# Three small cuts in the start-up of a token-mixing kernel: bands in one VectorE instruction, one evacuation moved to ScalarE, a weight load moved to a quiet step

## The chip, the cores and the metric

The kernel runs on one core of one Trainium2 chip. The metric is the device time of one execution in microseconds (us). The program's own span, which the profile counts from, is about 2 us shorter. Single runs of one and the same kernel lie up to some 5 us apart, and a good part of this study is about where that comes from. A "look" below is one profiled execution. To evacuate a tile is to copy a matmul's result out of PSUM, TensorE's accumulators, so that the next operation can use it.

## The reference, cut to what matters

A causal convolution of seven taps with softmaxed weights per head, then a token-mixing block:

```python
x_unf = x_pad[:, idx, :].reshape(B, S, K, H, group)      # B=8, S=4224, K=7, H=8, D=192
x = np.einsum('hk,bskhg->bshg', w, x_unf).reshape(B, S, D)
theta = x @ w_theta                                      # 192 x 192
zr, zi = x * np.cos(theta), x * np.sin(theta)
y = np.einsum('ts,bsd->btd', w_tok_r, zr) + np.einsum('ts,bsd->btd', w_tok_i, zi)   # 4224 x 4224
u = x + y
out = u + np.maximum(u @ w_ch, 0.0)
```

Nearly all arithmetic is in the two token matmuls.

## The kernel before

The tokens are cut into 33 chunks of 128. A chunk goes through `conv` (matmuls with banded weights), `transpose`, `theta` (a matmul and two sines on ScalarE), products and sums (VectorE), and is then one right-hand side of the token matmuls, which run in steps. In the start-up, about 100 us, eleven chunks are prepared while steps 0 to 4 already use those that are ready. After that TensorE is full. Filler matmuls (`idle`) on zeros are meant to raise TensorE's clock early on; "full" and "half" clock below are what the trace records as granted. The parts that the change and the argument touch:

```python
def transpose(self):
    self.xT = turned()
    transposed(self.xT, self.x, range(NG), self.k < 3)   # True: evacuated by VectorE, else ScalarE
...
# in mix(): the token matmuls of one step, seven runs, three PSUM accumulators in two buffers
for r, (wn, zn, cn, opens, to) in enumerate(runs):
    if opens:
        y[cn] = ypool.tile([P, 2, PC], F32, name="y", tag="y")
...
# start of the program, after the softmax of the taps
idle(8)
bp = banks("bp")
for q in range(Q): ...                                   # 32 tiny matmuls spread the taps into bp
bv = bp[0 : 2 * WR, 0, 0 : Q * H].rearrange("p (q h) -> p h q", h=H)
dve(nc.vector.tensor_scalar_mul(
    out=bands[:, :, 0, :], in0=bv, scalar1=block[:, 0:1]
))
act(nc.scalar.activation(
    out=bands[:, :, 1, :], in_=bv, func=AT.Copy, scale=block[:, 1:2]
))
...
# emitted after the eleven chunks of the start-up
dve(nc.vector.memset(wch[:, 1:3, :], 0.0))
for rows, i, part_w in channel_pieces(moe_w_ch):
    nc.gpsimd.dma_start(out=wch[rows, i, :], in_=part_w)
```

## Time and profile before

| | before |
|---|---|
| time, median of the runs made with the changed kernel | 1449.35 us (1445.97 to 1450.87, 4 runs) |
| span of the profiled run | 1449.8 us |
| TensorE idle in that span | 31.8 us |
| first convolution | 9.20 us |
| first sine on ScalarE | 15.94 us |
| end of the start-up: first token matmul after TensorE's last long wait | 103.82 us |

The two lines of the page that matter are the busy shares of the engines and the chain of waits that ended last, by engine:

```profile
PE 1418.0 (98%) x9809; PEld 887.4 (61%) x9809; DVE 976.5 (67%) x1051; ACT 315.2 (22%) x379; POOL 434.2 (30%) x655
...
PE 86%; DVE 5%; DMA 4%; ACT 2%; issue 2%; POOL 1%; SPq 0%; DVEq 0%; ACTq 0%; POOLq 0%
```

TensorE (PE) is busy for 98% of the span, and 86% of the chain is its own. The idle time lies mainly in the start-up (17.5 us before 104 us) and in the last 75 us (9.7 us), with 2.0 us of waits near 600 us. The prediction below shows the start-up's lines.

### The profile page before, as it was taken

The page shows a single profiled execution, that of the slowest core. Times are in us where ns is not written, and L with a number is a line of the kernel's source. Part 1 is how long each engine was busy: PE and PEld are TensorE (multiplying, and loading weights), DVE is VectorE, ACT ScalarE, POOL GpSimd, SP SyncE. Part 2 cuts the span into 40 slices and gives each one's busy share as a digit, 9 for nine tenths or more (in the row PEclk, how much of TensorE's full clock was granted, in tenths as well). Part 3 has the DMA queues.
Part 4 walks back from the last instruction along what each step waited for, and adds up shares of the span by engine and source line. Part 5 has one row for each costly group of instructions (what it writes and reads, how often), then busy time and mean ns, then how long its engine had stood idle before and what let it go on. Part 6 is the DMA issues. An engine that isn't in the chain of part 4 may idle for free.

```text
span 1449.8 us, 23748 instructions
## 1 busy us (share of the span) xinstructions
PE 1418.0 (98%) x9809; PEld 887.4 (61%) x9809; DVE 976.5 (67%) x1051; ACT 315.2 (22%) x379; POOL 434.2 (30%) x655
## 2 busy tenths in 40 slices
PE   7899999999999999999999999999999999999997
PEld 4556666666666666556666666666666666666665
DVE  6883555545448777756665667877777767767686
ACT  6851101111134244000000004434210110010133
POOL 7431211111233232342433342333323123213120
PEclk9999999999999999999999999999999999999999
DMA  9986756465699999988899889989999999999883
GB/s 171 246 164 140 146 101 151 89 149 97 137 232 206 223 249 217 227 222 209 206 267 210 237 143 240 238 184 230 279 216 210 206 200 223 204 204 194 166 227 119
DMA packets 272029, 281.99 MB, mean 195 GB/s; under 512 B 106672, under 2 KB 240176, under 8 KB 271920
## 3 DMA queue, kind: packets, MB, share of 16 engines
q0 software_dynamic: 162464, 92.15, 48.3%
q1 hardware_dynamic: 71824, 178.88, 35.0%
q10 hardware_dynamic: 37632, 9.44, 4.4%
q8 instruction: 77, 1.26, 0.3%
q14 instruction: 32, 0.26, 0.1%
HBM read 245.49 MB, written 108.13 MB: 244 GB/s over the span
## 4 chain that ended last, share of the span: by engine, by line
PE 86%; DVE 5%; DMA 4%; ACT 2%; issue 2%; POOL 1%; SPq 0%; DVEq 0%; ACTq 0%; POOLq 0%
PE y L443 78%; PE v L141 5%; DMA st<-in_moe_w_tok_i_dram 2%; PE pc L210 1%; PE tp L165 1%; DVE pv L408 1%; ACT z L246 1%; DVE z L257 1%; DVE z L251 1%; DVE wt L336 1%; DMA xw<-in_x_dram 1%; DVE wt L348 1%; ACT pv L406 1%; ACT uT L151 0%; DMA part<-pv 0%
## 5 line engine op out<-in xcount | busy, mean ns | idle before, releaser
L443 PE MATMUL y<-z,wt 128*128 128x384 f16 x7656 | 1285.6, 326 | 11.8 <-DVE pv L408 8.7
L443 PEld LDWEIGHTS <-wt 128*128 128x128 f16 x7656 | 741.1, 98 | 491.4 <-issue 14.4
L408 DVE TENSOR_TENSOR pv<-y,pv 128x768 f32<-128x768 f32 x324 | 308.9, 954 | 326.8 <-PE y L443 285.8
L336 DVE STREAM_TRANSPOSE wt<-st 128x1408 f16<-128x1408 f16 (+7 forms) x224 | 327.7, 1465 | 50.6 <-PE y L443 41.1
L323 POOL DMA_DIRECT2D st<-in_moe_w_tok_r_dram x232 | 132.3, 578 | 462.5 <-DVE wt L336 456.6
L323 POOL DMA_DIRECT2D st<-in_moe_w_tok_i_dram x232 | 132.3, 578 | 409.9 <-DVE wt L336 394.4
L348 DVE TENSOR_TENSOR wt<-wt 128x1408 f16<-128x1408 f16 (+7 forms) x216 | 174.1, 806 | 42.0 <-PE y L443 39.6
L151 ACT ACTIVATE z<-pc 128x768 f16<-128x768 f32 x65 | 53.3, 819 | 388.8 <-PE pc L210 388.6
L151 ACT ACTIVATE ub<-pv 128x768 f16<-128x768 f32 x63 | 50.2, 835 | 333.0 <-DVE pv L408 326.6
L406 ACT ACTIVATE pv<-y 128x768 f32<-128x768 f32 x66 | 54.0, 818 | 283.5 <-PE y L443 281.4
L141 PEld LDWEIGHTS <-uT 128*128 128x128 f16 x1056 | 91.5, 98 | 27.8 <-issue 9.0
L386 POOL TENSOR_TENSOR pv<-pv,xr 128x1536 f32<-128x1536 f32 x24 | 74.5, 3103 | 74.6 <-DVE wt L348 31.8
L197 POOL DMA_DIRECT2D xw<-in_x_dram x132 | 76.3, 586 | 26.9 <-DMA xw<-xw 7.5
L476 DVE SCALAR_TENSOR_TENSOR pv<-v,pv 128x768 f32<-128x768 f32 x66 | 62.9, 954 | 27.7 <-PE v L141 27.3
L257 DVE TENSOR_TENSOR z<-z 128x768 f16<-128x768 f16 x132 | 73.4, 556 | 3.6
L151 ACT ACTIVATE uT<-tp 128x1536 f16<-128x1536 f16 (+1 forms) x48 | 58.2, 1215 | 74.7 <-PE tp L165 74.7
L246 ACT ACTIVATE z<-v,half_pi 128x768 f16<-128x768 f32 x66 | 59.8, 906 | 42.5 <-PE v L141 42.1
L251 DVE TENSOR_TENSOR z<-z 128x1536 f16<-128x1536 f16 x66 | 60.1, 947 | 5.7 <-ACT z L246 5.7
L141 PE MATMUL v<-wth,uT 128*128 128x192 f16 x528 | 55.2, 248 | 5.7 <-ACT z L246 3.4
L141 PE MATMUL v<-wch,uT 128*128 128x192 f16 x528 | 54.2, 246 | 2.1 <-DVE pv L476 1.2
L246 ACT ACTIVATE z<-v 128x768 f16<-128x768 f32 x66 | 53.4, 810 | 0.0
L210 PE MATMUL pc<-xw,bands 96*64 96x192 f16 x528 | 35.7, 259 | 1.8 <-ACT bands L625 1.1
(44 smaller groups left out, 140.3 us busy)
## 6 DMA issues: line engine op xcount, KB each, us to landing
part<-pv SPq DMA_DIRECT2D x79, 768.0 KB, 4.3
pv<-part SPq DMA_DIRECT2D x79, 768.0 KB, 6.1
out_dram<-pv SPq DMA_DIRECT2D x66, 384.0 KB, 4.4
st<-in_moe_w_tok_r_dram POOLq DMA_DIRECT2D x136, 176.0 KB, 5.9
st<-in_moe_w_tok_i_dram POOLq DMA_DIRECT2D x136, 176.0 KB, 5.2
xs<-z SPq DMA_DIRECT2D x132, 96.0 KB, 4.2
xw<-in_x_dram POOLq DMA_DIRECT2D x121, 96.0 KB, 5.8
xr<-xs SPq DMA_DIRECT2D x24, 384.0 KB, 4.2
```

Source lines behind the costliest of these rows:

```text
L141: pe(nc.tensor.matmul(v[:, k, b * D : (b + 1) * D], lhsT=tT[:, 3 * k + b + i, :], rhs=w[:, 2 * b + i, :], start=(i == 0), stop=(i == 1),))
L151: act(nc.scalar.activation(out=out, in_=in_, func=AT.Copy))
L197: nc.gpsimd.dma_start(out=self.xw[lo : lo + n, h, :, :], in_=x[:, t0 : t0 + n, :].rearrange("b s d -> s b d"),)
L246: act(nc.scalar.activation(**args))
L251: dve(nc.vector.tensor_tensor(out=o, in0=xv, in1=o, op=ALU.mult))
L257: dve(nc.vector.tensor_tensor(out=z[:, o, :], in0=z[:, a, :], in1=z[:, b, :], op=ALU.subtract))
L323: pool(nc.gpsimd.dma_start(out=st[a * Q : (a + 1) * Q, 0:nb, :, 0:n] .rearrange("i r bt s -> i (r bt) s"), in_=w[self.tbs[0] * P : (self.t ...
L336: dve(nc.vector.transpose(self.w[name][:, 0 : self.n, :, :], self.st[int(name[1])][:, int(name[0]) - 1, :, 0 : self.n * Q] .rearrange("p b ...
L348: dve(nc.vector.tensor_tensor(out=self.w[name][:, 0 : self.n, :, :], in0=self.w[a][:, 0 : self.n, :, :], in1=self.w[b][:, 0 : self.n, :, : ...
L386: ins = pool(nc.gpsimd.tensor_tensor(out=self.pv[i], in0=self.pv[i], in1=self.xr[i], op=ALU.add))
L408: dve(nc.vector.tensor_tensor(out=o, in0=yv, in1=o, op=ALU.add))
L443: pe(nc.tensor.matmul(y[cn][:, q, 0:BH], lhsT=self.w[wn][:, c, :, :].rearrange("p bt i -> p (bt i)"), rhs=chunks[k].z[:, zn, q * BH : (q + ...
```

## The change

The intent is to shorten the start-up in three places: one VectorE instruction in place of a VectorE and a ScalarE instruction in a row, the transposed x of chunk 2 evacuated by ScalarE, which is idle there, and the zeroing and loading of the channel weights taken out of the start-up's full end and put into step 15, where there is room.

```diff
-            transposed(self.xT, self.x, range(NG), self.k < 3)
+            transposed(self.xT, self.x, range(NG), self.k < 2)
...
+        if t == NU - 2:
+            def load_wch():
+                dve(nc.vector.memset(wch[:, 1:3, :], 0.0))
+                for rows, i, part_w in channel_pieces(moe_w_ch):
+                    pool(nc.gpsimd.dma_start(out=wch[rows, i, :], in_=part_w))
+            found.append((3, load_wch))
...
-    dve(nc.vector.tensor_scalar_mul(
-        out=bands[:, :, 0, :], in0=bv, scalar1=block[:, 0:1]
-    ))
-    act(nc.scalar.activation(
-        out=bands[:, :, 1, :], in_=bv, func=AT.Copy, scale=block[:, 1:2]
+    dve(nc.vector.tensor_tensor(
+        out=bands, in0=bv.unsqueeze(2).to_broadcast([2 * WR, H, 2, Q]),
+        in1=block[:, :].unsqueeze(1).unsqueeze(3).to_broadcast([2 * WR, H, 2, Q]),
+        op=ALU.mult,
     ))
...
-    dve(nc.vector.memset(wch[:, 1:3, :], 0.0))
-    for rows, i, part_w in channel_pieces(moe_w_ch):
-        nc.gpsimd.dma_start(out=wch[rows, i, :], in_=part_w)
```

## The prediction

> **What bounds the kernel now.** I read the page's busy shares first, then the busy time of each engine by stretches, then the chain of waits, then the timeline of the few microseconds that the change touches. TensorE is busy for 1418.0 of 1449.8 us, so some 32 us can be lost or won in waits at all. The stretches show where they lie (columns: stretch and length, then busy us and instruction count of PE, PE weight loads, DVE, ACT and POOL, then the granted clock, DMA share, GB/s):
>
> ```profile
> 28.00:60.00 32.00, 26.50 (x244) 17.00 (x242) 26.77 (x43) 27.71 (x35) 17.60 (x32) 0.95 1.29 219
> 60.00:80.00 20.00, 18.41 (x179) 12.62 (x178) 19.26 (x28) 18.26 (x23) 6.80 (x12) 1.00 1.14 255
> 80.00:104.00 24.00, 20.65 (x163) 13.31 (x161) 22.24 (x31) 14.27 (x18) 6.49 (x12) 1.00 0.76 160
> 104.00:421.00 317.00, 317.00 (x1947) 190.28 (x1946) 159.79 (x140) 41.20 (x51) 66.40 (x117) 0.99 0.64 132
> ```
>
> From 104 to 421 us TensorE never waits. Before that there is a start-up of about 100 us in which eleven chunks of x go through convolution, transpose, sine and products while the first token matmuls already run. There ScalarE (27.71 of 32 us between 28 and 60) and then VectorE (22.24 of 24 us between 80 and 104) are the full engines. All three parts of the change remove work from that start-up, so they are worth only what they shorten of it; whatever TensorE gains there should shift the whole full stretch after it, and so the end.
>
> **Part one, the bands.** The timeline at the start:
>
> ```profile
> 8.10 0.48 DVE L622 TENSOR_SCALAR bands<-bp,block 96x256 f16<-96x256 f32 x1 [1.66 <-PE bp L616]
> ...
> 8.68 0.47 ACT L625 ACTIVATE bands<-bp,block 96x256 f16<-96x256 f32 x1 [1.90 <-DVE bands L622]
> ...
> 9.20 1.49 PE L210 MATMUL pc<-xw,bands 96*64 96x192 f16 x16 [1.14 <-ACT bands L625]
> ...
> 13.30 0.50 PEld L210 LDWEIGHTS <-bands 96*64 96x64 f16 x8 [0.20 <-DMA xw<-in_x_dram]
> ```
>
> Today VectorE writes one half of the bands, then ScalarE the other, one after the other (8.10 to 8.58, 8.68 to 9.15), and the first convolution starts at 9.20. After the change one VectorE multiply of 96 x 512 does both. The Trainium skill, "VectorE: DVE Perf Modes", in its perf-mode tier table has a tensor_tensor with a PSUM operand at one element per cycle, and in the section on the TRN2 errata gives (N+151)/0.96 ns for an fp32 tensor_tensor in SBUF. Applied to N = 768 that is 957 ns, and the trace has 954 ns for the 768-wide adds that read PSUM (L408), so it may be used here: N = 512 gives an estimated 0.69 us. Scaling from the 256-wide instruction instead (0.48 us plus 256 elements at 0.96 GHz) gives 0.75. The bands are then ready at 8.10 + 0.69..0.75 = 8.8 to 8.85 instead of 9.15: the first convolution starts **0.30 to 0.35 us earlier**.
>
> But what of it gets through? The last line shows TensorE at 13.30 waiting 0.20 us for a DMA, before the convolution of chunk 1. The instruction order shows the semaphores of that wait: the load of chunk 1 and the copies of its history rows out of chunk 0's tile, neither of which needs the bands. So the 0.3 us turns into a wait of 0.5 us there. The only other user, the evacuation of chunk 0's transposed x, moves earlier on VectorE and saves less than 0.1 us. I put this part at 0 to 0.1 us. The two casts of the theta weights behind it slip by about 0.25 us, to 9.5, and are first needed at 14.69.
>
> **Part two, the transposed x of chunk 2.** The timeline around it:
>
> ```profile
> 25.13 0.80 ACT L246 ACTIVATE z<-v 128x768 f16<-128x768 f32 x1
> ...
> 26.58 0.92 DVE L149 COPY uT<-tp 128x1536 f16<-128x1536 f16 x1
> 26.61 0.81 ACT L151 ACTIVATE z<-pc 128x768 f16<-128x768 f32 x1 [0.68 <-PE pc L210]
> 27.43 1.80 DVE L251 TENSOR_TENSOR z<-z 128x1536 f16<-128x1536 f16 x2
> ...
> 27.56 0.83 PE L141 MATMUL v<-wth,uT 128*128 128x192 f16 x8 [0.98 <-DVE uT L149]
> ...
> 28.43 0.90 ACT L246 ACTIVATE z<-v,half_pi 128x768 f16<-128x768 f32 x1 [1.00 <-PE v L141]
> ```
>
> The transposes are in PSUM at 25.13, but VectorE is busy with sums and a weight transpose and takes the tile only at 26.58. TensorE waits 0.98 us for it and ScalarE 1.00 us behind that. ScalarE is free from 25.93, and the order of the changed kernel puts the evacuation just there, ahead of the convolution output of 26.61. The Trainium skill, "ScalarE: Activation LUTs", section "What ACT_TABLE_LOAD costs", has an ACTIVATE with immediate scale and bias at 186 + 0.833 N ns and back-to-back ones overlapping by about 93 ns; for N = 1536 that is 1.47 us, and the trace has 1.45 to 1.50 us for the same evacuation on ScalarE in later chunks. So it ends at 25.93 + 1.45 = 27.38 to 27.43, against 26.58 + 0.92 = 27.50 on VectorE. The slower engine finishes first, by **about 0.1 us**, because it starts 0.65 us earlier. Its extra 1.35 to 1.45 us fit into the 0.68 + 1.00 = 1.68 us that ScalarE idles now. The displaced convolution output ends at 28.1, which frees its PSUM buffer just as TensorE wants it (28.2). From 28.43 the chain of waits runs mostly over ScalarE and TensorE up to about 58 us, so this 0.1 us should travel on. VectorE gets 0.92 us back, so the products at 27.43 move forward by some 0.8 us; but it idles 1.33 us for ScalarE at 43.60 and 1.80 at 50.35, which eats that. Sum: 0.1 us.
>
> **Part three, the channel weights.** The chain of waits ends its start-up on VectorE:
>
> ```profile
> 101.98 0.76 DVE wt L348
> 102.74 0.21 DVE wch L705
> 102.95 0.82 DVE pv L408
> 103.77 0.05 issue
> 103.82 6.24 PE y L443 x27
> ```
>
> This is the clearest piece. The zeroing of the channel-weight tile takes 0.21 us on a full VectorE immediately before the PSUM add for which TensorE waits 2.46 us. Taking it out lets TensorE resume **0.21 us earlier**, and TensorE does not wait again for 300 us. The four loads that hang on the memset blocked the GpSimd queue for 5.63 us, but the token-weight load behind them then waits 1.03 us more for a weight transpose anyway, so nothing is gained there. In their new place, step 15 (about 366 to 391 us), the queue stands idle: the trace has
>
> ```profile
> 387.42 2.28 POOL L323 DMA_DIRECT2D st<-in_moe_w_tok_i_dram  x4 [12.93 <-DVE wt L336]
> ```
>
> so 12.93 us of idle swallow four issues of 0.55 us = 2.2 us, and VectorE, idle for some 2 us between instructions there, swallows a 0.22 us memset. The Trainium skill, "DMA: Bandwidth & Descriptors", section "SWDGE vs HWDGE vs iDMA", says a cast during a DMA can only be issued from GpSimd, which is why this fp32 to fp16 load sits in that queue; the trace agrees (all wch issues are POOL's), and no other queue is tried here. The weights are first read at 1063 us. They could hardly be late.
>
> **Sum.** 0.05 + 0.1 + 0.21 = 0.36, so about **0.4 us of 1448, or 0.03%**. From the median of 1448.21 that is 1447.8.
>
> **Rivals.** First, **a new wait in the SyncE queue**. The built order shows one thing that the diff does not: the first load of x rows for the final sum (xr, 384 KB) moves from the 86th place of SyncE's queue to the 38th, ahead of the history copies of chunks 5 and 6, and it waits there for chunk 3's rows to land in DRAM. I estimate chunk 5's copies at 35.4 to 37.8 us instead of 32.45 to 34.9; with the 4.8 us from issue to landing that this stretch shows they are there at 42.6, and TensorE wants them at 44.3. DMA is full in this stretch, so the margin of under 2 us may not hold; a miss would cost perhaps 1 us, at most 3. It also rotates the semaphores and adds one or two waits to ScalarE's first accumulator copies (the trace has about 0.08 us for each). Second, **ScalarE as the tighter bound**: it is the fullest engine from 28 to 60 us and gets 1.35 us more. If the evacuation started later than 25.93, the convolution output behind it would hold the next matmuls and the part would lose up to 0.5 us. Against it stands the idle of 1.68 us. Third, **the gain is larger**: the earlier VectorE work could remove several later waits of TensorE, and the whole could reach 1.5 us. Against it: between 28 and 80 us ScalarE, not VectorE, ends most of the waits. Fourth, **everything is swallowed** but the memset, or even that, by a later wait (589 to 636 us on the token-weight loads): those start when TensorE lets VectorE transpose, so they should move with it.
>
> **Range and chances.** None of these reaches 29 us, which is what 2% would be. The regime-wise reading agrees with the Trainium skill, "Perfetto Trace Analysis", section "Optimization Strategy" (the most contended engine changes over time): only a stretch of 100 us is touched, and most of it is left as it is. The range is therefore mostly that of the runs: three of the same kernel span 1445.97 to 1450.87, 4.9 us, ten times my effect. I take 1445.3 to 1450.3. Faster by over 2%: 0.3%; slower: 0.7%.
>
> **What would show it.** Right: one bands instruction of 0.69 to 0.75 us and the first convolution at about 8.9; a longer DMA wait, near 0.5 us, before chunk 1's convolution; the evacuation of chunk 2 on ScalarE at 25.9 and the theta matmuls at 27.45; TensorE's last start-up wait ending at about 103.4; the wch issues near 380 us with no new TensorE wait. Wrong: a TensorE wait for a DMA near 44 us, a start-up ending after 103.8 or before 102.8, or TensorE waits between 104 and 421 us. The trace may well show the 0.4 us where the run times cannot.

## The result, and the profile after

| | before | after |
|---|---|---|
| median of 4 runs | 1449.35 us (1445.97 to 1450.87) | 1448.3 us (1446.65 to 1450.9) |
| span of the profiled run | 1449.8 us | 1444.6 us |
| first convolution | 9.20 | 8.89 |
| first sine | 15.94 | 14.74 |
| end of the start-up | 103.82 | 102.48 |

The ratio is 0.9998 with a 95% interval of 0.9973 to 1.0022: the same. A ratio is the mean time of one kernel's runs over that of the other's of the same rounds, so it is not quite the ratio of the medians.

But the two profiled runs differ by 5.2 us, 14 times what was predicted, and that needs an explanation before any part of it is credited to the change. The lines of the changed kernel that answer to those of before, first the page:

```profile
PE 1414.5 (98%) x9809; PEld 886.3 (61%) x9809; DVE 978.2 (68%) x1050; ACT 316.2 (22%) x379; POOL 434.6 (30%) x655
...
PE 89%; DVE 3%; DMA 2%; ACT 2%; POOL 1%; issue 1%; SPq 0%; DVEq 0%; ACTq 0%; POOLq 0%
```

The bands and what follows, from the timeline:

```profile
8.16 0.69 DVE L628 TENSOR_TENSOR bands<-bp,block 96x512 f16<-96x512 f32 x1 [1.66 <-PE bp L622]
...
8.89 1.49 PE L210 MATMUL pc<-xw,bands 96*64 96x192 f16 x16 [0.78 <-DVE bands L628]
...
12.68 0.52 PE L210 MATMUL pc<-xw,bands 96*64 96x192 f16 x8
```

The instruction takes 0.69 us, as estimated, and the first convolution starts 0.31 us earlier. The convolution of chunk 1, which was to wait 0.5 us for a DMA, waits for nothing and is 0.62 us earlier than before.

The transposed x of chunk 2:

```profile
24.62 1.45 ACT L151 ACTIVATE uT<-tp 128x1536 f16<-128x1536 f16 x1
...
25.95 0.82 ACT L151 ACTIVATE z<-pc 128x768 f16<-128x768 f32 x1
26.13 0.83 PE L141 MATMUL v<-wth,uT 128*128 128x192 f16 x8 [0.75 <-ACT uT L151]
...
27.00 0.90 ACT L246 ACTIVATE z<-v,half_pi 128x768 f16<-128x768 f32 x1 [0.23 <-PE v L141]
```

ScalarE takes it right behind the previous sine. The end of the start-up, from the chain of waits (start, length, engine and line), now without the memset:

```profile
100.80 0.76 DVE wt L348
101.55 0.88 DVE pv L408
102.43 0.05 issue
102.48 7.65 PE y L443 x46
```

And the channel weights in their new place, in the timeline; the bracket says for what GpSimd had waited before the line:

```profile
376.03 0.22 DVE L531 MEMSET wch<- 128x192 uint32 x1
376.55 1.61 POOL L533 DMA_DIRECT2D wch<-in_moe_w_ch_dram  x3 [4.47 <-DVE wch L531]
...
384.41 2.32 POOL L323 DMA_DIRECT2D st<-in_moe_w_tok_i_dram  x4 [6.25 <-DVE wt L336]
```

GpSimd still waits 6.25 us for VectorE afterwards, and TensorE has no wait between 104 and 421 us. So the move is hidden.

What then makes 5.2 us? Three pieces can be read off. The start-up ends 1.34 us earlier. Between 570 and 640 us the kernel before waited 1.97 us for token weights, and the changed one did not. The remaining 1.9 us lie mostly just after the start-up, and the stretches there show what they are (columns as in the prediction; the first number after POOL's count is the granted clock). The kernel before:

```profile
12.00:15.00 3.00, 3.00 (x25) 2.14 (x24) 1.59 (x3) 0.81 (x1) 3.00 (x6) 0.50 1.28 170
...
104.50:107.50 3.00, 3.00 (x11) 1.36 (x10) 2.04 (x3) 0.00 (x0) 2.16 (x4) 0.50 0.39 37
```

and the changed kernel:

```profile
12.00:15.00 3.00, 2.83 (x35) 1.96 (x35) 1.93 (x4) 1.07 (x2) 3.00 (x6) 0.95 1.34 180
...
104.50:107.50 3.00, 3.00 (x20) 1.80 (x19) 3.00 (x4) 0.26 (x1) 1.78 (x4) 1.00 0.84 108
```

In both stretches the kernel before ran at half the TensorE clock, 0.50 where the other has 0.95 and 1.00. In the second it did 11 matmuls in the time of 20. The clock record of the traces is a row of windows of 3.413 us each, at full or at half speed. Before: half from 8.66 to 15.48 (two windows), from 35.96, and from 104.23. After: half from 8.87 to 12.28 (one window) and from 36.17. So two fewer half-speed windows. Is that the change, or chance?

### The profile page after: what moved, and what is told of

Read it like the earlier page. It is cut to its first block, busy times and chain, and to the rows that moved or that the text cites. A ratio compares the mean times of both kernels' runs of the same rounds, so it can differ in the third digit from the quotient of the medians.

```text
span 1444.6 us, 23749 instructions
## 1 busy us (share of the span) xinstructions
PE 1414.5 (98%) x9809; PEld 886.3 (61%) x9809; DVE 978.2 (68%) x1050; ACT 316.2 (22%) x379; POOL 434.6 (30%) x655
## 4 chain that ended last, share of the span: by engine, by line
PE 89%; DVE 3%; DMA 2%; ACT 2%; POOL 1%; issue 1%; SPq 0%; DVEq 0%; ACTq 0%; POOLq 0%
PE y L443 81%; PE v L141 5%; PE pc L210 1%; PE tp L165 1%; ACT z L246 1%; DVE pv L408 1%; DMA xw<-xw 1%; POOL xw L197 1%; DMA xw<-in_x_dram 1%; DVE z L257 1%; POOL st L323 1%; DVE z L251 1%; DMA pv<-part 1%; ACT uT L151 1%; DVE wt L336 0%
## 5 line engine op out<-in xcount | busy, mean ns | idle before, releaser
L348 DVE TENSOR_TENSOR wt<-wt 128x1408 f16<-128x1408 f16 (+7 forms) x216 | 176.1, 815 | 40.5 <-PE y L443 38.0
```

Source lines behind the costliest of these rows:

```text
L348: dve(nc.vector.tensor_tensor(out=self.w[name][:, 0 : self.n, :, :], in0=self.w[a][:, 0 : self.n, :, :], in1=self.w[b][:, 0 : self.n, :, : ...
```

## The experiments

**Theory A**: the parts of the change set the start-up, and a second look at either kernel gives the same figures. **Theory B**: the boundaries of the clock windows lie elsewhere in each run, so which windows come out at half speed is partly chance; the parts are worth a few tenths each on top. A third question is whether the bands' 0.31 us passes on or is swallowed by a DMA, as predicted.

Looks compare stretches of one trace, not total times.

### A second look at the kernel before

No edit.

> The kernel before, unchanged, a second look. In the first look its clock record has half-speed windows of 3.41 us: two in a row from 8.66 us, one at 35.96, one at 104.23; the start-up ended at 103.82 and the first ScalarE sine at 15.94. Theory A (the parts of the change alone set the start-up): the same figures within 0.1 us. Theory B (the clock windows lie where they happen to, and their number differs from run to run): the phase of the windows is different, the number of half-speed windows before 110 us need not be four, and the first sine lies between 14.9 (one early window) and 16.0 (two), the start-up end moving with it.

Measured: span 1446.4 us, 3.4 us less than the first look at the same program, and its first sine and start-up end differ by 0.22 and 0.46 us. Theory A is out. The bands matmuls took 2.64 us in place of 1.57, because the fillers had not raised the clock by then; full clock came at 13.88 us. First convolution 10.28, first sine 16.16, start-up end 104.28, all later than in the first look. But no half-speed window followed at 104 us and there was no wait near 600. The first sine is 0.16 us above the expected range of 14.9 to 16.0: the early clock has more than the two cases that were thought of.

### One part at a time

```diff
 bands only : tensor_scalar_mul + activation  ->  one tensor_tensor        (rest as before)
 xT only    : self.k < 3  ->  self.k < 2                                   (rest as before)
 wch only   : memset and loads moved to step 15                            (rest as before)
```

> Before plus part one only (one VectorE instruction for the bands). Theory A (prediction): first convolution 0.31 us earlier (8.9), but the convolution of chunk 1 waits for a DMA until about 13.3, first sine at 15.9, start-up end 103.7 to 103.8. Theory C (the 0.31 us passes through because no DMA gates chunk 1): chunk 1 at 13.0 with equal clock, first sine 15.6, start-up end about 103.5. Theory B (an early half-speed window lost or kept decides): first sine near 14.8 if only one early half-speed window is recorded, near 15.6 to 15.9 if two.

> Before plus part two only (transposed x of chunk 2 evacuated by ScalarE). Prediction: up to the second chunk nothing changes; the interval from the first sine of chunk 1 to the first sine of chunk 2 (21.82 to 28.43 in the first look, 6.61 us) becomes about 6.5 by the prediction, 6.38 as the look at the changed kernel had it. Both theories: by chunk 3 (first look: sine at 39.77, that is 17.95 after chunk 1's) the changed kernel had lost it again (17.95): if the loss belongs to the part, it is lost here too.

> Before plus part three only (channel weights loaded in step 15). From the last sine of the start-up (93.17) to the first matmul after the last start-up wait (103.82) it takes 10.65 us in the first look. Prediction: 10.44, as the memset of 0.21 us is gone; the changed kernel had 10.50. Rival (the memset had slack): 10.65. Nothing at 370 to 380 us makes TensorE wait.

Measured, bands only: first convolution 8.85, chunk 1 at 12.66 with no DMA wait, first sine 14.72, start-up end 102.86. One early half-speed window, as theory B had it; whether the 0.35 us as such passes on is told below, by all looks together.

Measured, transposed x only: from the second sine of chunk 1 to the first sine of chunk 2 it takes 3.87 us (24.78 to 28.65). The second look at before has 4.10 (24.55 to 28.65), bands only 4.10, wch only 4.10, and the changed kernel 3.87. The lines of the second look at before and of xT only, in this order:

```profile
26.80 0.92 DVE L149 COPY uT<-tp 128x1536 f16<-128x1536 f16 x1
...
28.65 0.90 ACT L246 ACTIVATE z<-v,half_pi 128x768 f16<-128x768 f32 x1 [1.00 <-PE v L141]
```

```profile
26.27 1.45 ACT L151 ACTIVATE uT<-tp 128x1536 f16<-128x1536 f16 x1
...
28.65 0.90 ACT L246 ACTIVATE z<-v,half_pi 128x768 f16<-128x768 f32 x1 [0.23 <-PE v L141]
```

So the part gains **0.23 us**; all eight looks at the changed kernel and its variants have 3.86 or 3.87. The old place can cost more: in w_before (below), where VectorE first waited 0.81 us for a token-weight DMA and so took the tile late, the interval is 5.00 us. That is one look, so how often it happens is not known. From the first sine of chunk 1 it takes 6.38 us, as expected from the look at the changed kernel. The gain is not lost by chunk 3: the interval from 24.78 to chunk 3's first sine is 15.36, against 15.67 in the second look at before. That the first look had suggested a loss fits the clock again: its half-speed window near 36 us lies at another place in the work.

Measured, channel weights only: from the last sine of the start-up to its end 10.50 us against 10.64 to 10.66 in the three others. The line of TensorE's wait in the second look at before and in this one, in this order:

```profile
104.28 3.91 PE L443 MATMUL y<-z,wt 128*128 128x384 f16 x23 [2.46 <-DVE pv L408]
```

```profile
104.34 3.91 PE L443 MATMUL y<-z,wt 128*128 128x384 f16 x23 [2.31 <-DVE pv L408]
```

The wait is 2.31 in place of 2.46: **0.15 us**, not the 0.21 of the memset. VectorE's lines show where the rest went, again the second look at before first:

```profile
103.20 0.22 DVE L705 MEMSET wch<- 128x192 uint32 x1
103.33 0.90 DVE L408 TENSOR_TENSOR pv<-y,pv 128x768 f32<-128x768 f32 x1
```

```profile
101.79 1.62 DVE L348 TENSOR_TENSOR wt<-wt 128x1152 f16<-128x1152 f16 x2
103.33 0.95 DVE L408 TENSOR_TENSOR pv<-y,pv 128x768 f32<-128x768 f32 x1
```

In both the add starts 0.08 us before the instruction ahead of it ends. Counted from the end of the last weight sum (L348, 103.21 and 103.41), it starts 0.12 us after it with the memset and 0.08 us before it without, so the whole 0.21 us is saved at its start. But the add then takes 0.95 us in place of 0.90, in each of three looks without the memset (this one, the changed kernel, and the changed kernel in five rounds) against each of four with it. Why it is longer behind the weight sum than behind the memset is not shown.

### Trying to hold the clock

```diff
 # zero tile of the fillers written first, so that they start at 1.2 us and not 2.4
-    idle(8)
+    idle(16)
 ...
+    idle(4)      # between the 32 bands matmuls and their evacuation
 # a third kernel besides: the bands instruction of w_after issued twice
```

> The kernel before with more filler matmuls at the very start: the zero tile they read is written first (filler from about 1.3 us instead of 2.4), 16 instead of 8 of them, and 4 more between the bands matmuls and the first convolution. Theory B (clock windows of 3.41 us with a chance phase decide most of the early difference): full clock from 4 to 7.1 us at nearly every phase, bands matmuls 1.57 us and not 2.64, at most one early half-speed window, first sine at or before 15.3, start-up end at or before 103.4, where the three looks at cold starts had 104.3. Theory A (clock unimportant): first sine 15.9 to 16.4 as before. The time: 0.5 to 1.5 us less than before, not to be told from its spread.

> The changed kernel with the same added filler. If the three parts are worth 0.36, 0.23 and 0.15 us at equal clock, as the single looks suggest, the start-up ends 0.74 us before that of w_before with the same clock windows, and the first sine lies 0.36 us earlier. By the prediction (a DMA swallows the bands' gain) the first sine is the same and the end 0.36 us earlier. Start-up end 102.3 to 102.7.

> w_after with the bands instruction issued twice, so that the bands are ready 0.6 to 0.69 us later. By the prediction (0.3 us is swallowed before chunk 1, that is, chunk 1 does not wait for the bands) the first sine moves by at most 0.4 us. If the bands gate everything, by the whole 0.6 to 0.69 us, or more where an extra half-speed clock window comes with it; the convolution of chunk 1 shows no wait for a DMA.

> The changed kernel, a second look. Theory B: with a cold start (bands matmuls 2.64 us) the start-up ends 0.74 us before the 104.3 of the cold looks at the kernel before and its single parts, so near 103.5; with an early warm clock near 102.5 as in its first look. Theory A: 102.5 in any case. From the end of the start-up to the end of the program about 1342.1 us in both, unless a half-speed window falls just after the last start-up wait (1.7 us more) or TensorE waits for token weights between 570 and 640 us (2 us more).

Measured: the early filler did raise the clock in all three, at 5.09, 4.11 and 4.47 us. But the window after the one in which the bands matmuls began came out at half speed, and in two of the three the next one too, so the clock was not held. w_before: first sine 14.68, start-up end 103.58, which misses the expected 103.4 at most; VectorE's late evacuation of chunk 2, named above, took 0.90 us there. w_after: 15.88 and 102.67; the four fillers ran at half speed, took 1.46 us and pushed its own first convolution to 9.73. With the bands instruction twice the first convolution is at 9.68, no later than in w_after, since in w_after the fillers and not the bands were last. So this pair says nothing about the bands, and w_after against w_before cannot be read as intended. The timed ratios to before are 0.9986 (0.9970 to 1.0002) and 0.9987 (0.9965 to 1.0010): same.

The second look at the changed kernel gave 14.76 and 102.49, span 1444.6, like its first look: it had by chance the same early clock (full from 5.82, one half window from 9.23).

### Cold starts, and filler in the last wait

```diff
 # c_after: the changed kernel without the fillers at its start
-    idle(8)
 # f_after: twelve fillers in front of a run that opens an accumulator (t == 4; corrected to 3 in f2_after)
+    if self.t == 4 and r == 5:
+        fill = banks("fill")
+        for _ in range(12):
+            pe(nc.tensor.matmul(fill[:, 0, 0 : 2 * D], lhsT=ident, rhs=wth[:, 0:2, :]..., start=True, stop=True))
```

> The changed kernel without the eight filler matmuls at its start, so that TensorE is at half clock until the first full window of convolution work, as it was by chance in three looks with the old bands (first convolution at 10.28 to 10.32, full clock from 13.88 to 14.52, first sine 16.16 to 16.41, start-up end 104.25 to 104.34). Here the first convolution should start at 9.92 (0.36 us earlier). If the bands' gain passes through at equal clock: first sine 15.8 to 16.05 and start-up end 103.5 to 103.7 (0.36 + 0.23 + 0.15 less). If a DMA swallows it before chunk 1, as predicted: first sine 16.1 to 16.4 and start-up end 103.9 or later.

> The changed kernel with twelve filler matmuls (2.0 us) in the last wait of the start-up, 100.2 to 102.5 us, where TensorE waits for VectorE. In four looks that wait lay inside one clock window and a half-speed window of 3.41 us followed, at 1.7 us of loss; in six looks it straddled two windows and none followed. With the filler no half-speed window between 100 and 110 us at any phase, start-up end at 102.5 to 102.7, and the time without the 1.7 us of the unlucky runs: on average 0.3 to 0.7 us less than the changed kernel. If idle TensorE is not what sets the clock, a half-speed window can still follow. It might show at most as 0.2 to 0.3% below before.

> The changed kernel once more, timed in five rounds. If the parts are worth 0.74 us at equal clock and the rest is chance, the ratio to the kernel before is 0.9995 with half a per mille either way, which no number of rounds here resolves against a spread of about 5 us; the interval includes 1. Each run's span should be the start-up end plus 1342.1 us, or 1.7 to 3.7 us more, so between 1444.5 and 1449.

> The filler of f_after put where the wait is (f_after had it one step too late, 21 us after the wait, where TensorE is full: against c_after, which by chance had the same clock windows, it cost just its 2.0 us). Now twelve filler matmuls stand in step 3 before the run that opens the third accumulator, so in the 2.3 us in which TensorE waits for VectorE. If TensorE's idleness inside one window is what halves the clock after it: TensorE idle at most 0.4 us there, start-up end unchanged (102.5 to 104.4 by the early clock), no half-speed window between 100 and 110 us, and from the start-up end to the end of the program 1342.1 us, without the 1.7. On average over runs 0.5 to 0.8 us below the changed kernel, which five rounds may not resolve. If a half-speed window still follows, theory B's reading of the late window falls.

Measured, cold start: first convolution 9.96, but full clock only at 16.25, first sine 16.77, start-up end 104.35. The first sine misses both expected ranges, and the end fits only the "or later" of the second, since the clock came one window later than I had assumed; so this run decides between them only by the comparison at equal clock below. Its line before chunk 1 is of use:

```profile
14.05 0.50 PEld L210 LDWEIGHTS <-bands 96*64 96x64 f16 x8 [0.20 <-issue]
```

It is the same gap of 0.20 us that the prediction had read as a wait for a DMA, here put down to nothing.

Measured, f_after: the filler stood in the wrong step and ran at 125 us, where TensorE is full. It happened to have the clock windows of c_after (full from 16.28 and 16.25), and its span is 1450.10 against 1448.13: it cost 1.97 us, its twelve matmuls' 2.0, and shows that outside a wait a filler is paid in full. Its ratio is 1.0019 (1.0002 to 1.0035).

Measured, the changed kernel in five rounds: ratio 0.9998, interval 0.9986 to 1.0010. Its profile was a cold start (bands matmuls 2.64 us) with full clock from 13.08: first convolution 9.93, first sine 15.66, start-up end 103.39, span 1445.5.

Measured, f2_after: the filler ran in the wait, and no half-speed window followed:

```profile
100.00 2.11 PE L439 MATMUL fill<-wth,ident 128*128 128x384 f16 x12
102.47 9.76 PE L451 MATMUL y<-z,wt 128*128 128x384 f16 x59 [0.35 <-DVE pv L408]
```

TensorE's wait shrank to 0.35 us with the end of the start-up unchanged at 102.47. Five runs lay between 1446.63 and 1448.42 us, ratio 0.9989 (0.9975 to 1.0003): not told from before. And the profiled run's windows lay so that no half-speed window was due without the filler either (two looks with nearly these windows had none). So the filler's benefit is not shown.

### All looks together

| look | first conv. | full clock from | first sine | sine minus conv. | start-up end | half window at 103 to 105 | span minus start-up end |
|---|---|---|---|---|---|---|---|
| before | 9.20 | 15.48 | 15.94 | 6.74 | 103.82 | yes | 1345.99 |
| before, second | 10.28 | 13.88 | 16.16 | 5.88 | 104.28 | no | 1342.08 |
| xT only (old bands) | 10.31 | 14.33 | 16.39 | 6.08 | 104.25 | no | 1342.27 |
| wch only (old bands) | 10.32 | 14.52 | 16.41 | 6.09 | 104.34 | no | 1342.04 |
| w_before (old bands) | 9.24 | 11.91 | 14.68 | 5.44 | 103.58 | yes | 1343.71 |
| bands only | 8.85 | 12.54 | 14.72 | 5.87 | 102.86 | no | 1341.82 |
| after | 8.89 | 12.28 | 14.74 | 5.85 | 102.48 | no | 1342.10 |
| after, second | 8.89 | 12.64 | 14.76 | 5.87 | 102.49 | no | 1342.12 |
| after, five rounds | 9.93 | 13.08 | 15.66 | 5.73 | 103.39 | no | 1342.09 |
| c_after | 9.96 | 16.25 | 16.77 | 6.81 | 104.35 | yes | 1343.78 |
| f_after | 9.96 | 16.28 | 16.79 | 6.83 | 104.38 | yes | 1345.72 |
| f2_after | 8.86 | 12.52 | 14.73 | 5.87 | 102.47 | no | 1342.25 |
| w_after | 9.73 | 14.35 | 15.88 | 6.15 | 102.67 | yes | 1345.54 |
| w_bands_twice | 9.68 | 14.71 | 15.87 | 6.19 | 103.16 | yes | 1343.81 |

(All in us; "full clock from" is the end of the half-speed windows around the first convolutions.)

Three things follow. First, **the bands' gain passes on**. The time from first convolution to first sine depends on how long the clock stays at half after that convolution, and old and new bands lie on one curve: with 3.60 us of it the old bands need 5.88, with 3.69 and 3.75 the new need 5.87; with 6.28 the old need 6.74, with 6.29 the new 6.81. Nothing swallows 0.3 us in between. Nor later: from first sine to start-up end it takes 88.14 us with bands only and 88.12 in the second look at before (87.88 in the first, with its clock windows elsewhere). The time from the start of the evacuation of the bands to the first convolution is 1.10 us with the old bands in all four looks without added filler, 0.73 to 0.75 with the new: **0.36 us** at equal clock.

Second, **after the start-up all looks are alike**: 1341.8 to 1342.3 us to the end, and 1.7 us more where one half-speed window follows at 103 to 105 us (half of 3.41 us lost), plus what is named: the token-weight wait of 1.97 us in the first look at before and of 1.43 in w_after, 2.0 us of misplaced filler in f_after. At most 0.3 us is left over.

Third, **when that window comes is regular**. TensorE's last start-up wait is 2.3 to 2.5 us long. In the six looks with a half-speed window the whole wait lay inside one clock window, the one just before. In the seven others with that wait it was cut by a boundary, and no window held more than 1.66 us of it. Where the boundary lies differs from run to run of one program. This is regular for this wait alone. Near 36 us, windows in which TensorE was idle for 1.6 to 2.4 us were followed by half speed in 13 looks, while in w_after one with 1.76 us (31.41 to 34.83) was not. So idle time alone is not the rule.

## Why the prediction was right, and where its steps were not

The time, 1448.3 against 1447.8 forecast, came out; so did the reason that the range is that of the runs. The sum underneath was half of what was measured. With runs 4.9 us apart any sum from nothing to a few us would have passed, so the hit says nothing for the steps; that the total still fell so near is luck.

**Part one, the bands.** The instruction's estimate (0.69 to 0.75) and the earlier convolution (0.30 to 0.35) hold: 0.69, and 0.36 at equal clock. The step "turns into a wait of 0.5 us" for a DMA before chunk 1 failed, and with it "0 to 0.1 us". A gap of 0.19 to 0.20 us at this place appears in eight looks, put down to a DMA in three and to "issue" in five, and in all eight it begins while TensorE is at half clock. In the five looks with full clock there it is 0.10 to 0.11 us, too short for the timeline to show it; in bands only, where the clock changes just after the gap begins, 0.15. A gap that halves when TensorE's clock doubles belongs to the slow clock and not to a DMA. In the changed kernel chunk 1 starts at 12.68, so the data had landed by then. The term should have been 0.36.

**Part two, transposed x.** ScalarE takes the tile early and its extra time fits in its idle time, as predicted; the displaced convolution output delays nothing. The term was mis-sized: 0.23 us, not 0.1. The prediction compared ends only as read off the two engines (27.38 to 27.43 against 27.50). In the trace of xT only the next sine waits 0.23 us for TensorE where it had waited 1.00, and the matmuls start 0.06 us after the 1.45 us evacuation, which itself began 0.69 us after the 0.80 us sine before it, overlapping it. In the first look's times that is an end at 25.13 + 0.69 + 1.45 = 27.27, which is 0.23 us before 27.50. The prediction named the overlap of activations in a row but let the evacuation start when the sine ends.

**Part three, channel weights.** The place on the path is right, the size 0.15 in place of 0.21, since the add behind it became 0.05 to 0.06 us longer. The prediction's chain has 0.82 us for that add, the chain of the changed kernel 0.88. The new place is hidden, as predicted; GpSimd's wait behind it is 6.25 us long.

**Sum.** 0.36 + 0.23 + 0.15 = 0.74 us at equal clock, in place of 0.36. The start-up ends agree: the changed kernel in its two early looks is 0.37 to 0.38 us ahead of bands only, which are the other two parts. And with a cold start, 103.39 against 104.28 is 0.89, of which 0.74 is the parts and the rest an earlier full clock.

**The rivals.** The new wait in SyncE's queue did not come: the xr load was issued at 33.05 us, and the convolution near 43 us waited 0.22 us for ScalarE, not for a DMA. ScalarE as tighter bound did not come either. "The gain is larger" is what happened, by a factor of two, for another reason than the one given.

**What was not seen at all** is the clock. The prediction took the first trace of before as the kernel's behaviour, although four half-speed windows in it were partly chance, and read one gap made by them as a DMA. Two of its own signs fell out against it: the DMA wait of 0.5 us before chunk 1 did not come, and the start-up ended at 102.48, "before 102.8", which it had named as a sign of being wrong. The second sign is a poor one: with the same start-up code the end lies between 102.48 (after) and 104.38 us (f_after), by the clock. One thing is left open: the earlier convolution may also raise the chance that the window after it is busy enough to be followed by full clock. At nearly the same windows (boundaries at 8.66 and 8.87 us) the old bands had two half windows and the new one, worth another 0.9 us; but the boundaries are not the same, and no run could fix them.

## What to carry to other kernels

Before a difference of a microsecond between two profiles is explained by a change, look twice at the same kernel, and compare intervals between named instructions instead of spans. Ask of each short wait beside a slow clock whether the clock made it. And measure the gain of removing an instruction between fixed neighbours: the one behind it may start earlier by the whole of it and then take longer.

## What the Trainium skill lacked or had wrong

- "TensorE: Matmul & The Clock Gate", Part 1, says that the clock's activity window is 4096 cycles or 3413 ns, free-running, and that cold starts therefore vary from run to run; the traces agree (windows of 3.41 us, full clock first from 4.11 to 16.28 us in 14 looks). It gives a return to half clock "after ≥1 idle window (~3.4µs)". Here less was enough: the window with the last start-up wait, idle for 2.3 to 2.5 us, was followed by half speed in six looks of six, and windows near 36 us, idle for 1.6 to 2.4 us, in 13. But one idle for 1.76 us was not (w_after, 31.41 to 34.83).
- The same page puts the ramp penalty under 1% of a typical span and advises not to fit a count of cold matmuls. The first holds here: one half-speed window costs 1.7 us of 1448. But that is more than twice the 0.74 us of this change, so it is not to be left out when small changes are compared.
- The same page does not say how much of a window must be busy. A window with 2.74 us of 128 x 128 filler matmuls was followed by full clock (5.24 us, before). One with 2.88 us, half of it the 96 x 64 convolution and most of the rest filler, was not (12.84 us, c_after), nor was one with 2.75 us, of which 1.57 were the tiny bands matmuls (8.50 us, w_before). So busy time alone does not decide it; what does is open.
- "VectorE: DVE Perf Modes", section on the TRN2 errata, gives (N+151)/0.96 ns for an fp32 tensor_tensor. It held for one operand in PSUM and the other broadcast, and an fp16 result: 0.69 us at N = 512.
